# Fused forgetting attention and SwiGLU FFN: q and k of the first four head pairs in two column parts, their first gate sums by TensorE, and a new order of the first loads

## The chip, the cores and the metric

The kernel runs on one core of a Trainium2 chip. The core has five engines with instruction streams of their own: TensorE (PE, matrix products), VectorE (DVE), ScalarE (ACT), GpSimd (POOL) and SyncE (SP, which here only issues transfers). Transfers between DRAM and the on-chip memory are issued by SP, ACT or POOL and carried by 16 DMA engines. The metric is device time in microseconds (us) of one execution; lower is better.

## The reference

Causal attention with a forget gate for 8 batches, 8 heads, 576 positions and head size 64, followed by a feed-forward block over the 4608 tokens of 512 features, inner size 1536.

```python
scores = q @ k.T / sqrt(64)
cum    = cumsum(log(clip(f, 1e-4, 1)), axis=-1)         # per batch and head
scores = where(causal, -1e9, scores + cum[:, :, :, None] - cum[:, :, None, :])
attn   = softmax(scores) @ v
x      = attn with the heads of a token side by side    # 4608 x 512
out    = (silu(x @ w_gate) * (x @ w_val)) @ w_out
```

In a row of the scores the term of the row itself is the same for every column and drops out of the softmax, so only the sums of the columns are added.

## The kernel before

The work unit of attention is a pair of heads, 32 in all, four per batch. A pair's 576 query rows are cut into nine blocks of 64. Blocks 0 to 3 are the pair's first half (g = 0), blocks 4 to 8 its second half (g = 1). Block i needs the first 64(i + 1) columns of k. The two heads of a pair stand side by side in the 128 rows of every score tile.

For each pair the kernel does the following. `load_pair` brings q and k in as float32 (`kf`, `qf`, two buffers each), k in 96 partitions and q in 72, one transfer each, together with the gate sums `cb`: two transfers, one per head, each spreading one row of 576 sums over 64 partitions. `prepare` casts k and q to bfloat16 (L438, L436, L434), has TensorE transpose them in six and eight pieces (L452) and copies the results out of PSUM into `kt` and `qz` (L464, L466); q's copies are two, one per head. `scores` lets TensorE multiply a block (L498) and add the causal mask through an identity product (L502). VectorE adds `cb` and takes the minimum of the row in one instruction (L526), ScalarE does the exponential and its sum (L546). `normalize` scales the weights to bfloat16 tiles `pk` on POOL (L582); for pairs 0 to 7 TensorE transposes them (L612, copied out at L617), for later ones a transposing DMA does. `weighted` multiplies them with v (`vt`, L638), and `spread` copies the result into `xT` (L662), the FFN's input, a ring of 2560 tokens.

v comes in five chunks of 128 rows per batch (`load_v`, L678), each for all heads, through the float32 buffers `vf`, of which there are two, and is cast to `vt` (L682). The weights of the FFN come through POOL's queue with a cast, in four column pieces each for `wg` and `wv` (L695) and three pieces for `wo` (L699).

The gate sums of all 64 head rows are made once in the tile `fa` (buffer `t`): clamp (L366), logarithm (L368) and running sum (L369). The sums are stored to DRAM (`cum_f`, L378) and every pair's `cb` is read back from there (L418). Only pair 0 (`NSEL = 1`) goes another way: `select` multiplies `fa` with a 0/1 matrix `one` on TensorE (L393, in float32) and copies the result to `cb` (L397).

The FFN works on token tiles, the first two of 256 tokens. 256 tokens are the first halves of the four pairs of a batch, so tile 0 needs g = 0 of pairs 0 to 3, and tile 1 takes in their second halves. `gate` (L720) streams the tokens against `wg` and `wv`, ScalarE and VectorE combine them (L726, L728, L731), `project` (L748) multiplies with `wo`, and ScalarE or VectorE copies out (L755, L757).

The order on every engine is planned at build time. Each operation is declared with `pl.op`: engines it may run on with an assumed cost, the keys it reads and writes, a priority. `Plan.order` is a list scheduler: it takes the operation that can start soonest by its model and gives buffers in turn. `HEAD` lists the order of the first eight halves as pair and half, `at` holds each half's place in it, `NUDGE` shifts priorities of single units, `STARTUP` gives the order of the first loads: `p3` is q and k of pair 3, `f9` the gates, `c2` the sums of pair 2, `v01` chunk 1 of batch 0, `wv4` the piece of `wv` that starts at 128-column block 4. The load with number n in that list waits for the one that is `AHEAD` places ahead, and POOL's for the one `BEHIND` places ahead; within a queue transfers go out in order, so that one which waits for its buffer holds the ones behind it.

Of the kernel before, what the change touches and what calls it, by code (L numbers as in the profile page):

```python
# [194 lines left out]
def mm(*cols):  # L195
    return sum(max(29, c / 2.4 + 2.5) for c in cols)
# [3 lines left out]
def kernel(  # L200
# [46 lines left out]
    NDIRECT = 0  # L247
    NSEL = 1
    MOST = (("p", 1), ("o", 2), ("f", 3))
    AHEAD = 7  # L250
# [13 lines left out]
    NUDGE = "a10.0:1 a13.0:2 a15.0:-1 a15.1:-0.5 a16.1:-2 a20.0:-1 a21.0:1 a23.1:-1 a26.1:0.5 a27.1:-1.5 a28.0:1 a29.0:1 a31.1:10 f3:-4 f4:-7 f5:1 f6:2 f7:4.5 f8:4 f9:8 o6:-2.5 o8:2 q11:-2 q15:4 q22:5.5 q24:2.5"  # L264
# [34 lines left out]
    bufs("cm", [P, NB, QB], F32, 2)  # L299
# [11 lines left out]
    bufs("vf", [P, H, D], F32, 2)  # L311
# [24 lines left out]
    one = sb.tile([BH, 2 * max(NSEL, 1), 64], F32)  # L336
    setup({"POOL": 160 + 110 * NSEL}, lambda e: nc.gpsimd.tensor_copy(one, ident[0:BH, 0:2 * max(NSEL, 1)].unsqueeze(2).to_broadcast((BH, 2 * max(NSEL, 1), 64))),
# [36 lines left out]
    for p in range(NDIRECT):  # L374
# [5 lines left out]
    pl.op({"ACT": 1400}, lambda e: nc.scalar.activation(tiny[:, 1:2], tiny[:, 0:1], AF.Exp),  # L380
          [(("cb", p), 2) for p in range(NDIRECT)] + [("fa", 2), "ln"], ["exp"], -95)


    def select(p):
        pl.key(("cb", p), "cb", p)
        for n in range(2):
            a, z = S // 2 * n, S // 2 * (n + 1)
            bk = ("cs", p, n)
            pl.key(bk, "gv", line="c")

            def mult(e, p=p, bk=bk, a=a, z=z):
                w = one[:, 2 * p:2 * p + 2, :].rearrange("b h r -> b (h r)")
                nc.tensor.matmul(pl.buf(bk)[:, 0:z - a], w, pl.buf("fa")[0:BH, a:z], start=True, stop=True)  # L393
            pl.op({"PE": mm(4 * (z - a))}, mult, [("fa", 3), "one"], [bk], -98.5 + 3 * p, lat=220, holds=["fa"])

            def evac(e, p=p, bk=bk, a=a, z=z):
                (nc.scalar.copy if e == "ACT" else nc.vector.tensor_copy)(pl.buf(("cb", p))[:, a:z], pl.buf(bk)[:, 0:z - a])  # L397
            pl.op({"ACT": 370, "DVE": 385}, evac, [bk], [("cb", p), (("cb", p), 3)], -98.5 + 3 * p)
# [70 lines left out]

    def epool(i):  # L470
        return f"e{i}" if i % 2 == 0 else "eo"
# [13 lines left out]
    def scores(p, g):  # L485
# [3 lines left out]
        for n, bank in enumerate(BANKS[g]):  # L489
# [14 lines left out]
            pl.op({"PE": mm(*cols)}, mult, [("kt", p), ("qz", p), (("kt", p), "done"), (("qz", p), "done"), "mask"], [sk], pr, lat=220)  # L504
# [8 lines left out]
            for i, a, z in cuts:  # L513
# [18 lines left out]
                r = [sk, ("cm", p) if own else (("cb", p), 3)] + ([("m", p, i, "part")] if a and not two else [])  # L532
# [337 lines left out]
```

## Time and profile before

| | |
|---|---|
| median of 3 runs | 420.01 us (419.38 to 426.64) |
| the profiled execution | 420.02 us |
| its span, first to last instruction | 418.2 us |
| PE busy | 398.1 us (95%) |
| DVE busy | 325.3 us (78%) |
| ACT busy | 311.0 us (74%) |
| POOL busy | 252.6 us (60%) |
| first score matmul | 13.72 us |
| first add of gate sums on DVE (L526) | 17.63 us |
| first FFN matmul (L720) | 34.83 us |
| moved by DMA | 72.22 MB, mean 173 GB/s |

A page of the profile shows one execution. Its second part cuts the span into 40 slices of 10.5 us and gives each engine's busy share in tenths. Its chain follows the last instruction back to what released it, step by step. An answer on windows gives, for each stretch, the busy time of each engine and the number of its instructions in brackets, then the granted TensorE clock, the DMA share and the rate in GB/s. A timeline row has start, duration, engine, line, operation, tiles written and read, and in square brackets the idle time ahead of it with what ended it. SPq, ACTq and POOLq rows are issues of transfers: their duration is the issuing engine's, not the transfer's. Busy time of PE is modelled from pipelined instructions and is no measure of how much it streams.

### The profile page before, as it was taken

The page shows a single profiled execution, that of the slowest core. Times are in us where ns is not written, and L with a number is a line of the kernel's source. Part 1 is how long each engine was busy: PE and PEld are TensorE (multiplying, and loading weights), DVE is VectorE, ACT ScalarE, POOL GpSimd, SP SyncE. Part 2 cuts the span into 40 slices and gives each one's busy share as a digit, 9 for nine tenths or more (in the row PEclk, how much of TensorE's full clock was granted, in tenths as well). Part 3 has the DMA queues.
Part 4 walks back from the last instruction along what each step waited for, and adds up shares of the span by engine and source line. Part 5 has one row for each costly group of instructions (what it writes and reads, how often), then busy time and mean ns, then how long its engine had stood idle before and what let it go on. Part 6 is the DMA issues. An engine that isn't in the chain of part 4 may idle for free.

```text
span 418.2 us, 9999 instructions
## 1 busy us (share of the span) xinstructions
PE 398.1 (95%) x3304; PEld 231.8 (55%) x3304; DVE 325.3 (78%) x1044; ACT 311.0 (74%) x875; POOL 252.6 (60%) x460
## 2 busy tenths in 40 slices
PE   1679999999999999999999999999999999999996
PEld 1446887665555555555555555555454444447875
DVE  4589999989998979889998979898866474553532
ACT  4689999999999978888987979899886332223321
POOL 7399977999788983886795787759784000000000
PEclk9999999999999999999999999999999999999999
DMA  7999999997999999999999999979976401001111
GB/s 176 203 166 235 220 214 206 224 236 183 204 229 212 232 197 237 204 237 199 225 216 226 228 235 210 234 189 208 221 155 146 88 2 51 25 27 50 52 52 52
DMA packets 143029, 72.22 MB, mean 173 GB/s; under 512 B 117761, under 2 KB 129793, under 8 KB 142977
## 3 DMA queue, kind: packets, MB, share of 16 engines
q1 hardware_dynamic: 136804, 66.27, 73.8%
q0 software_dynamic: 5808, 4.72, 7.7%
q10 hardware_dynamic: 364, 0.59, 0.6%
q8 instruction: 26, 0.43, 0.4%
q14 instruction: 27, 0.21, 0.2%
HBM read 47.04 MB, written 9.58 MB: 135 GB/s over the span
## 4 chain that ended last, share of the span: by engine, by line
PE 77%; DMA 7%; ACT 6%; POOL 4%; DVE 3%; issue 2%; SPq 0%; POOLq 0%; DVEq 0%; ACTq 0%
PE gv L720 38%; PE gv L748 20%; PE sp L498 8%; PE tx L638 5%; DMA kf<-in_k_dram 3%; PE tx L452 3%; POOL pk L582 3%; PE gv L612 2%; DMA pT<-pk 2%; DVE t L526 2%; ACT eo L546 2%; ACT e L546 2%; PE sp L502 1%; DMA cb<-cum_f 1%; DMA cum_f<-t 1%
## 5 line engine op out<-in xcount | busy, mean ns | idle before, releaser
L526 DVE CUSTOM_DVE_ANT_0 t<-sp,cb 128x512 f32<-128x512 f32 (+7 forms) x288 | 130.9, 475 | 13.5 <-PE sp L502 5.0
L582 POOL TENSOR_SCALAR pk<-e,lr 128x128 bf16<-128x128 f32 (+3 forms) x190 | 100.1, 530 | 32.7 <-DVE lr L564 15.1
L720 PE MATMUL gv<-xT,wv 128*128 128x512 bf16 (+2 forms) x576 | 111.4, 326 | 0.0
L720 PE MATMUL gv<-xT,wg 128*128 128x512 bf16 (+2 forms) x576 | 111.3, 326 | 0.0
L728 DVE SCALAR_TENSOR_TENSOR th<-th,gv 128x512 f32<-128x512 f32 x108 | 73.9, 685 | 43.7 <-ACT th L726 43.2
L748 PE MATMUL gv<-wo,hh 128*128 128x512 bf16 (+1 forms) x444 | 107.5, 374 | 0.0
L726 ACT ACTIVATE th<-gv 128x512 f32<-128x512 f32 x108 | 64.0, 592 | 42.1 <-PE gv L720 40.3
L546 ACT ACTIVATE e<-t,tm 128x448 f32<-128x448 f32 (+4 forms) x160 | 88.5, 555 | 4.6 <-DVE tm L526 3.9
L731 DVE TENSOR_TENSOR hh<-th,gv 128x512 bf16<-128x512 f32 x108 | 73.4, 685 | 9.0 <-PE gv L720 5.5
L498 PE MATMUL sp<-kt,qz 128*128 128x448 bf16 (+6 forms) x320 | 72.8, 295 | 3.8 <-DVE tm L526 3.7
L582 POOL TENSOR_SCALAR pk<-eo,lr 128x256 bf16<-128x256 f32 (+3 forms) x128 | 67.7, 530 | 12.4 <-DVE lr L564 4.9
L546 ACT ACTIVATE eo<-t,tm 128x256 f32<-128x256 f32 (+3 forms) x128 | 71.2, 557 | 4.3 <-DVE tm L526 2.2
L720 PEld LDWEIGHTS <-wv 128*128 128x128 bf16 x576 | 49.3, 98 | 34.8
L720 PEld LDWEIGHTS <-wg 128*128 128x128 bf16 x576 | 49.2, 98 | 35.0
L748 PEld LDWEIGHTS <-hh 128*128 128x128 bf16 x444 | 39.7, 98 | 37.1
L502 PE MATMUL sp<-mask,ident 128*128 128x64 bf16 x288 | 48.2, 197 | 0.0
L755 ACT ACTIVATE ot<-gv 128x512 f32<-128x512 f32 (+1 forms) x33 | 19.1, 581 | 36.7 <-PE gv L748 34.7
L498 PEld LDWEIGHTS <-qz 128*128 128x128 bf16 x320 | 31.0, 101 | 19.8 <-DVE qz L466 1.3
L436 POOL TENSOR_SCALAR qb<-qf 72x1024 bf16<-72x1024 f32 x30 | 31.2, 1041 | 8.8 <-DMA qf<-in_q_dram 6.1
L502 PEld LDWEIGHTS <-ident 128*128 128x128 bf16 x288 | 27.2, 100 | 15.2 <-issue 3.9
L546 ACT ACTIVATION_READ_ACCUMULATOR e<-t,tm 128x1 f32 x160 | 30.7, 192 | 0.0
L638 PE MATMUL tx<-pT,vt 128*64 128x320 bf16 (+4 forms) x448 | 29.4, 266 | 0.7 <-DMA pT<-pk 0.3
(60 smaller groups left out, 379.7 us busy)
## 6 DMA issues: line engine op xcount, KB each, us to landing
out_dram<-ot SPq DMA_DIRECT2D x35, 256.0 KB
kf<-in_k_dram SPq DMA_DIRECT2D x31, 288.0 KB
qf<-in_q_dram SPq DMA_DIRECT2D x31, 288.0 KB
cb<-cum_f SPq DMA_DIRECT2D x62, 144.0 KB
vf<-in_v_dram SPq DMA_DIRECT2D x32, 256.0 KB
wo<-in_moe_w_out_dram POOLq DMA_DIRECT2D x3, 512.0 KB, 9.2
vf<-in_v_dram SPq DMA_DIRECT2D x8, 128.0 KB
wv<-in_moe_w_val_dram POOLq DMA_DIRECT2D x2, 512.0 KB, 8.3
```

The costliest lines, as they stand in the source:

```text
L436: eng[e].tensor_scalar(dst, src, -scale, 1.0, op0=ALU.mult, op1=ALU.mult)
L498: nc.tensor.matmul(sp[:, o:o + z - a], qz[:, i, :, :].rearrange("p h r -> p (h r)"), kt[:, a:z], start=True, stop=not last or p >= MFROM)
L502: nc.tensor.matmul(sp[:, o - QB:o], ident, mask, start=False, stop=True)
L526: nc.vector.tensor_tensor_reduce(out=pl.buf(tk)[:, a:z], in0=pl.buf(sk)[:, o:o + z - a], in1=pl.buf(("cm", p))[:, i, :] if own else pl.buf ...
L546: nc.scalar.activation(pl.buf(ek)[:, :L], pl.buf(tk)[:, :L], AF.Exp, bias=pl.buf(("tm", p, g))[:, 0, i:i + 1], scale=-1.0, accum_out=pl.bu ...
L582: eng[e].tensor_scalar(dst, src, r, 1.0, op0=ALU.mult, op1=ALU.mult)
L638: nc.tensor.matmul(xo[r, 0:QB * n], vt[:, c, 2 * hp + h, :], pT[:, a:a + n, 64 * h:64 * h + 64], start=(c == 0), stop=(c == nch - 1))
L720: nc.tensor.matmul(pl.buf(bk)[:, j * n:j * n + n], wt[:, ko, fc * P:fc * P + P], xT[:, ko, x0:x0 + n], start=ko == 0, stop=ko == KD - 1)
L726: pl.op({"ACT": 487}, lambda e, u=u: nc.scalar.activation(pl.buf(("th", t, u)), pl.buf(("wg", t, u)), AF.Tanh, scale=0.5), [("wg", t, u)], ...
L728: pl.op({"DVE": 605}, lambda e, u=u: nc.vector.scalar_tensor_tensor(pl.buf(("th", t, u)), pl.buf(("th", t, u)), 1.0, pl.buf(("wg", t, u)), ...
L731: pl.op({"DVE": 605}, lambda e, u=u: nc.vector.tensor_mul(pl.buf(("hh", t, u)), pl.buf(("th", t, u)), pl.buf(("wv", t, u))), [("u", t, u), ...
L748: nc.tensor.matmul(pl.buf(bk)[:, 0:z - a], hh[:, (fc % nf) * n + ms * P:(fc % nf) * n + ms * P + P], wo[:, fc, a:z], start=fc == 0, stop=f ...
```

## The change

The columns of q and k of pairs 0 to 3 are cut at `CUT` = 256 into part A (blocks 0 to 3) and part B (the other 320 columns). `parts` lists the pieces. For pairs 0 and 1 together, and 2 and 3 together, part A of k, part A of q and part B of k are one piece each, with the two pairs one below the other in the partitions (64 each); part B of q is a piece per pair (80 partitions). `load_parts` issues one transfer per pair and piece, part A of pairs 0 and 1 from ACT and the others from SP. `prepare_parts` casts a piece in one instruction, transposes it in four or five pieces and copies each pair's share out. A first half waits for parts A alone, a second half for both (`pair_done`, `cb_done`).

`select` now takes one part: part A of the gate sums of pairs 0 to 3 (`NSELA`) and part B of pair 0 come from TensorE; part B of pairs 1 to 3 is read back from DRAM, 320 columns instead of 576. The matrix `one` grows from 2 to 8 head rows.

The first eight halves start with pair 0 instead of pair 1; the second halves stay in the order 1, 0, 3, 2. The first loads have a new order, in which `k0` and `q1` are parts B, and `AHEAD` is 10 instead of 7. An unused pool `cm` goes, `vf` has three buffers instead of two, the load of the exponential's table gets a bias of 1000 in the planner, and `NUDGE` has new values throughout the kernel.

```diff
     JFROM = 8
     TWO = True
     NDIRECT = 0
+    NHALF = 4
+    NSELA = 4
     NSEL = 1
+    CUT = QB * (HI[0] + 1)
     MOST = (("p", 1), ("o", 2), ("f", 3))
-    AHEAD = 7
+    AHEAD = 10
     BEHIND = 6
     BOTH = 8
     LATER = {"DVE": 100}
@@ -257,11 +262,11 @@
...
-    STARTUP = "p0 f9 p1 c1 p3 p2 c2 v00 c3 wv0 wg2 wg0 wv2 v04 wv4 v01 v03 c4 wg4 v02 p4 wg8 wv8 v10 f0 p5 p6 c5 v14 c6 wo0 p7 wo4 v12 v13 v11 c7 wo8"
-    HEAD = "10 00 20 30 11 01 31 21"
...
+    STARTUP = "p0 f9 k0 p2 wv0 wg0 c0 v01 q1 q0 wv2 wg2 c1 v02 v00 k2 v04 c3 q2 wv4 v03 wg4 q3 c2 p4 v11 c4 wg8 wv8 c5 v14 p5 v13 v12 p6 c7 v10 c6 wo0 wo4 wo8 p7"
+    HEAD = "00 10 20 30 11 01 31 21"
...
-    bufs("cm", [P, NB, QB], F32, 2)
...
-    bufs("vf", [P, H, D], F32, 2)
+    bufs("vf", [P, H, D], F32, 3)
...
-    one = sb.tile([BH, 2 * max(NSEL, 1), 64], F32)
-    setup({"POOL": 160 + 110 * NSEL}, lambda e: nc.gpsimd.tensor_copy(one, ident[0:BH, 0:2 * max(NSEL, 1)].unsqueeze(2).to_broadcast((BH, 2 * max(NSEL, 1), 64))),
+    one = sb.tile([BH, 2 * NSELA, 64], F32)
+    setup({"POOL": 160 + 110 * NSELA}, lambda e: nc.gpsimd.tensor_copy(one, ident[0:BH, 0:2 * NSELA].unsqueeze(2).to_broadcast((BH, 2 * NSELA, 64))),
...
-    pl.op({"ACT": 1400}, lambda e: nc.scalar.activation(tiny[:, 1:2], tiny[:, 0:1], AF.Exp),
...
-    def select(p):
...
+    o.bias = {"ACT": 1000}
+    def select(p, part, a, z):
+        bk = ("cs", p, part)
+        pl.key(bk, "gv", line="c")
+        def mult(e):
+            w = one[:, 2 * p:2 * p + 2, :].rearrange("b h r -> b (h r)")
+            nc.tensor.matmul(pl.buf(bk)[:, 0:z - a], w, pl.buf("fa")[0:BH, a:z], start=True, stop=True)
+        pr = at[p, 0] - 1.2 if part == "A" else at[p, 1] - 1
+        pl.op({"PE": mm(4 * (z - a))}, mult, [("fa", 3), "one"], [bk], pr, lat=220, holds=["fa"])
+        def evac(e):
+            (nc.scalar.copy if e == "ACT" else nc.vector.tensor_copy)(pl.buf(("cb", p))[:, a:z], pl.buf(bk)[:, 0:z - a])
+        pl.op({"ACT": (z - a) * .833 + 130, "DVE": (z - a) / .96 + 85}, evac, [bk], [("cb", p), (("cb", p), part)], pr)
+    def cb_done(p, g):
+        return [(("cb", p), x) for x in ("A", "B")[:g + 1]] if p < NHALF else [(("cb", p), 3)]
+    def pair_done(p, g):
+        if p >= NHALF:
+            return [("kt", p), ("qz", p), (("kt", p), "done"), (("qz", p), "done")]
+        return [(("kt", p), x) for x in ("A", "B")[:g + 1]] + [(("qz", p), x) for x in ("A", "B")[:g + 1]]
...
+        if p < NHALF:
+            load_parts(p)
+            return
...
-        if NDIRECT <= p < NSEL:
-            select(p)
-        elif p >= NSEL:
+        if p >= NSEL:
...
+        if p < NHALF:
+            prepare_parts(p)
+            return
...
+    def parts(p):
+        if p % 2 == 0:
+            yield "k", "A", 0, CUT, 4, 2
+            yield "q", "A", 0, CUT, 4, 2
+            yield "k", "B", CUT, S, 5, 2
+        yield "q", "B", CUT, S, 4, 1
+    def load_parts(p):
+        b, hp = divmod(p, NPB)
+        pl.key(("cb", p), "cb", p)
+        for name, x, a, z, r, n in parts(p):
+            fk = (name + "f", p, x)
+            pl.key(fk, name + "f")
+            m = (z - a) // r
+            def load(e, fk=fk, src=(k if name == "k" else q), a=a, z=z, r=r, n=n, m=m):
+                for u in range(n):
+                    h0 = 2 * (hp + u)
+                    (nc.scalar if e == "ACT" else nc.sync).dma_start(
+                        out=pl.buf(fk)[m * u:m * u + m, :, 0:r * D],
+                        in_=src[b, h0:h0 + 2, a:z].rearrange("h (p r) d -> p h (r d)", r=r))
+            loads[name, p, x] = pl.op({"ACT" if p == 0 and x == "A" else "SP": 550 * n}, load, (), [fk], -99 + 3 * p, dma=n * (z - a) * 2)
+        for x, a, z, sel in (("A", 0, CUT, NSELA), ("B", CUT, S, NSEL)):
+            if p < sel:
+                select(p, x, a, z)
+                continue
+            for h in range(2):
+                loads["cb", p, x, h] = pl.op({"SP": 600}, lambda e, h=h, a=a, z=z: nc.sync.dma_start(
+                    out=pl.buf(("cb", p))[64 * h:64 * h + 64, a:z],
+                    in_=cum_dram[2 * p + h:2 * p + h + 1, a:z].to_broadcast((64, z - a))),
+                    ["cum_dram"], [(("cb", p), x)], -98.5 + 3 * p, dma=z - a, holds=[("cb", p)])
+    def prepare_parts(p):
+        for name, x, a, z, r, n in parts(p):
+            fk, bk, tk = (name + "f", p, x), (name + "b", p, x), ("tt", name, p, x)
+            m = (z - a) // r
+            pr = min(at[p + u, x == "B"] for u in range(n)) - 1 + (name == "q") * .1
+            pl.key(bk, name + "b")
+            pl.key(tk, "tx", line="q")
...
+            L = 2 * r * D
+            o = pl.op({"POOL": L + 60, "ACT": L * .833 + 210, "DVE": L * .62 + 60}, cast, [fk], [bk], pr)
+            o.bias = SPARE if p else {}
+            oks = [(("kt" if name == "k" else "qz"), p + u) for u in range(n)]
+            if x == "A":
+                for ok in oks:
+                    pl.key(ok, ok[0])
+            def transpose(e, bk=bk, tk=tk, r=r, w=m * n):
+                src = pl.buf(bk).rearrange("p r h d -> p r (h d)")
+                for j in range(r):
+                    nc.tensor.transpose(half(tk)[:, w * j:w * j + w], src[0:w, j, :], ident[0:w, 0:w])
+            pl.op({"PE": r * (m * n / 2.4 + 2.5)}, transpose, [bk], [tk] + (oks if x == "A" else []), pr, lat=200, holds=oks)
+            for u in range(n):
+                for lo, hi, h in ([(0, P, None)] if name == "k" else [(0, 64, 0), (64, 128, 1)]):
+                    def evac(e, lo=lo, hi=hi, h=h, u=u, tk=tk, ok=oks[u], a=a, z=z, r=r, n=n, m=m):
+                        src = half(tk)[lo:hi, 0:r * m * n]
+                        if h is None:
+                            src = src.rearrange("c (j u p) -> c u p j", j=r, u=n)[:, u, :, :]
+                            dst = pl.buf(ok)[lo:hi, a:z].rearrange("c (p j) -> c p j", j=r)
+                        else:
+                            src = src.rearrange("c (j u i p) -> c u i p j", j=r, u=n, i=(z - a) // QB)[:, u, :, :, :]
+                            dst = pl.buf(ok)[lo:hi, a // QB:z // QB, h, :].rearrange("c i (p j) -> c i p j", j=r)
+                        if e == "ACT":
+                            nc.scalar.copy(dst, src)
+                        else:
+                            nc.vector.tensor_copy(dst, src)
+                    pl.op({"ACT": (z - a) * .85 + 125, "DVE": (z - a) * 1.15 + 90}, evac,
+                          [tk] + ([("z", "qz", p + u)] if h is not None and p + u < len(pl.pools["qz"]) else []),
+                          [(oks[u], x)], at[p + u, int(x == "B")] - .9, holds=[oks[u]])
...
-            pl.op({"PE": mm(*cols)}, mult, [("kt", p), ("qz", p), (("kt", p), "done"), (("qz", p), "done"), "mask"], [sk], pr, lat=220)
+            pl.op({"PE": mm(*cols)}, mult, pair_done(p, g) + ["mask"], [sk], pr, lat=220, holds=[("kt", p), ("qz", p)])
...
-                r = [sk, ("cm", p) if own else (("cb", p), 3)] + ([("m", p, i, "part")] if a and not two else [])
+                r = [sk] + ([("cm", p)] if own else cb_done(p, g)) + ([("m", p, i, "part")] if a and not two else [])
...
+        elif x[0] == "p" and n < NHALF:
+            line += [loads["k", n, "A"], loads["q", n, "A"]]
+        elif x[0] in "kq":
+            line.append(loads[x[0], n, "B"])
+        elif x[0] == "c" and n < NHALF:
+            line += [loads["cb", n, y, h] for y in "AB" for h in range(2) if ("cb", n, y, h) in loads]
```

More of the change, by code (lines that the diff above doesn't have):

```diff
@@ L379 @@
           [("fa", 3)], ["cum_dram"], -120, dma=570, lat=0, holds=["fa"])
-    pl.op({"ACT": 1400}, lambda e: nc.scalar.activation(tiny[:, 1:2], tiny[:, 0:1], AF.Exp),
+    o = pl.op({"ACT": 1400}, lambda e: nc.scalar.activation(tiny[:, 1:2], tiny[:, 0:1], AF.Exp),
           [(("cb", p), 2) for p in range(NDIRECT)] + [("fa", 2), "ln"], ["exp"], -95)
-    def select(p):
[L385 to L398, printed above, removed]
+    o.bias = {"ACT": 1000}
[16 more added lines that the diff above has]
+        return [(("kt", p), x) for x in ("A", "B")[:g + 1]] + [(("qz", p), x) for x in ("A", "B")[:g + 1]]
     def half(key):
@@ new lines, in prepare_parts, with cast @@
+    def prepare_parts(p):
[5 more added lines that the diff above has]
+            pl.key(tk, "tx", line="q")
+            def cast(e, name=name, fk=fk, bk=bk, r=r, w=m * n):
+                src = pl.buf(fk)[0:w, :, 0:r * D].rearrange("p h (r d) -> p r h d", d=D)
+                dst = pl.buf(bk)[0:w, 0:r, :, :]
+                if e == "ACT":
+                    nc.scalar.activation(dst, src, AF.Copy, scale=-scale if name == "q" else 1.0)
+                elif name == "q":
+                    eng[e].tensor_scalar(dst, src, -scale, 1.0, op0=ALU.mult, op1=ALU.mult)
+                else:
+                    eng[e].tensor_copy(dst, src)
+            L = 2 * r * D
[20 more added lines that the diff above has]
+                            dst = pl.buf(ok)[lo:hi, a // QB:z // QB, h, :].rearrange("c i (p j) -> c i p j", j=r)
+                        if e == "ACT":
+                            nc.scalar.copy(dst, src)
+                        else:
+                            nc.vector.tensor_copy(dst, src)
+                    pl.op({"ACT": (z - a) * .85 + 125, "DVE": (z - a) * 1.15 + 90}, evac,
+                          [tk] + ([("z", "qz", p + u)] if h is not None and p + u < len(pl.pools["qz"]) else []),
+                          [(oks[u], x)], at[p + u, int(x == "B")] - .9, holds=[oks[u]])
```

2 lines of the change are left out of this document (1 added, 1 removed).

## The prediction

> **What bounds the kernel now.** I read the page first: its span, the slices and the chain's shares.
>
> ```profile
> span 418.2 us, 9999 instructions
> ...
> PE   1679999999999999999999999999999999999996
> ...
> GB/s 176 203 166 235 220 214 206 224 236 183 204 229 212 232 197 237 204 237 199 225 216 226 228 235 210 234 189 208 221 155 146 88 2 51 25 27 50 52 52 52
> ```
>
> TensorE looks full from the fourth slice on. A busy share is not work, so I set its work against its best pace. The longest single-line piece of the whole chain's list in mid-kernel gives that pace.
>
> ```profile
> 187.15 4.32 PE gv L720 x20
> ```
>
> 4.32 us for 20 matmuls of 512 columns is 216 ns each, 0.42 ns per column. The FFN streams 4608 x 96 gate columns and 36 x 12 x 512 projection columns: 186.6 + 93.3 us. Attention, by the loops of the code, has per pair 2880 score, 576 mask, 1152 transpose and 1600 effective PV columns (the two heads run side by side: ten PV matmuls of 320 columns take 0.71 us), 84 us for 32 pairs. The on-chip transposes of eight pairs add 10.8. That is 375 us of work in 418.2, so some 43 us are lost. The windows say where.
>
> ```profile
> core 0: us, PE busy (x) PEld busy (x) DVE busy (x) ACT busy (x) POOL busy (x), PEclk, DMA share, GB/s
> 0.00:5.00 5.00, 0.00 (x0) 0.00 (x0) 1.90 (x8) 1.49 (x2) 4.11 (x27) 1.00 0.62 151
> 5.00:10.00 5.00, 1.52 (x8) 1.24 (x9) 3.27 (x4) 3.11 (x4) 3.36 (x8) 1.00 0.79 191
> 10.00:15.00 5.00, 4.15 (x39) 2.95 (x38) 1.79 (x3) 2.90 (x5) 1.77 (x3) 1.00 0.82 214
> 15.00:20.00 5.00, 2.74 (x32) 2.20 (x30) 3.50 (x12) 2.55 (x9) 1.79 (x2) 1.00 1.17 211
> 20.00:25.00 5.00, 2.56 (x25) 2.16 (x24) 4.34 (x30) 4.71 (x20) 3.53 (x8) 1.00 1.43 164
> 25.00:30.00 5.00, 4.45 (x24) 2.29 (x24) 4.41 (x20) 4.60 (x18) 4.91 (x11) 1.00 0.92 156
> 30.00:35.00 5.00, 4.17 (x41) 2.29 (x41) 4.96 (x18) 4.59 (x16) 4.96 (x10) 1.00 1.16 210
> ```
>
> VectorE (third pair of figures) does almost nothing until 17.6 us and is full from about 20 on. The first gate matmul starts at 34.83. Until then TensorE has streamed 19,600 effective columns, which is 8.2 us of work, so 26.6 of the 43 lost us lie ahead of the first gate. The chain of waits over the first 36 us names what holds VectorE back:
>
> ```profile
> 1.38 6.10 DMA kf<-in_k_dram
> ...
> 8.81 3.11 DMA cum_f<-t
> ...
> 12.45 5.02 DMA cb<-cum_f
> ...
> 17.63 0.39 DVE t L526
> ```
>
> The gate sums go out to DRAM and come back repeated over 64 partitions, 8.81 to 17.47, although the scan that makes them ended at 7.80 and the first scores were done at 14.7. After 17.63 the chain is VectorE and ScalarE until 34.58, then TensorE. The timeline shows the rest that I use:
>
> ```profile
> 6.45 1.35 DVE L369 TENSOR_TENSOR_SCAN t<-tiny,t 64x576 f32<-64x576 f32 x1 [0.29 <-ACT t L368]
> ...
> 9.07 2.29 PE L393 MATMUL gv<-t,one 64*128 64x288 f32 x4
> ...
> 10.43 0.40 ACT L397 COPY cb<-gv 128x288 f32<-128x288 f32 x1 [1.55 <-PE gv L393]
> ...
> 15.64 9.65 SPq L678 DMA_DIRECT2D vf<-in_v_dram  x3
> ```
>
> The last row is SP held from 16.94 to 24.89 at the third v load: both v buffers were full, and the copy that frees one ran on POOL at 24.26.
>
> **The change, part by part.** *Gate sums by TensorE.* Columns 0 to 255 for pairs 0 to 3, 256 to 575 for pair 0. By L393, 2.29 us for 576 columns is 4.0 ns per column: 1.02 us for each A part, 1.27 for the B part, 5.4 in all against 2.29. It falls where TensorE is idle; without that cover it would cost 3.1. Pair 0's sums stand at 7.80 + 0.1 + 1.02 + 0.2 of latency + 0.36 of copy = 9.5.
>
> *Two parts of q and k.* A parts of two pairs share one load, cast and transpose group. Per two pairs the casts fall from 3584 to 2688 elements per partition, the transposed columns stay 2304. The copies out are split, twelve more of some 0.1 us each, 1.2 us over VectorE and ScalarE ahead of 34; I count them in the VectorE stretch below. The loads go from 8 to 16 DMAs on k and q. SP gets six more, at the 0.31 to 0.57 us that its k and q issues took about 3 us; ACT four instead of two, at 0.39 and 0.67 about 1 us, which puts its table load from 1.87 to 2.9 and its end to 4.4, before VectorE's clamp ends at 5.71: nothing, and beyond 1.3 us of slip one for one.
>
> *When the first add starts.* k and q A of pairs 0 and 1 and f are 0.67 MB. The present start moved 0.75 MB by 5.0 us (151 GB/s), so q is there at about 5.5. Cast (half of POOL's 1.04), four transposes of 128 (0.5) and six copies of 0.38 on two engines (1.1) end at 8 to 8.5, the scores at 9. So the sums are last, and the first add starts near 9.8 instead of 17.63.
>
> *What is late next.* Four first halves took VectorE from 17.63 to 25.8, 8.2 us; from 9.8 that ends at 18 if k and q A of pairs 2 and 3 are there. They wait on SP for the first k buffer (about 6), and share the wires with wv0 and wg0: in by 12.7. So the next bound is v: PV of every pair needs v00 and v01. By the new plan 4.9 MB stand ahead of the end of v00 (0.52 + 0.15 + 0.33 + 0.52 of q, k, f, four weight pieces of 0.52, v01, q1, q0, c1, v02, v00). The windows above sum to 4.66 MB at 25 and 5.44 at 30, so 4.9 MB were moved at 26.5. The third v buffer takes away SP's stop, in which the rate was 164 and 156: at 200 it would be 24.5. I take 25.5. The cast is 0.60 us, four PVs (0.36 warm, 0.55 for eight) 1.5, the last copies 0.7: first gate at 28.4, between 27.4 and 30.
>
> *What that is worth.* By then TensorE has done less: four first halves, their transposes, some 1.6 second halves, 16,400 effective columns, 6.9 us. Lost ahead of the gate: 28.4 - 6.9 = 21.5, against 26.6. That is 5.1 us won, 3.5 to 6.1 over the gate's range.
>
> *The clock.* Mask matmuls took 0.26 us until 29.04 and 0.19 from 30.03, groups of six transposes 0.83 and 0.50. The granted share in the windows is 1.00 throughout, so it does not show this. If the pace rises only after dense work, the first gates at 28.4 may run slow. Dense work began at 24.98, and the rise came 4.5 us later; gates at half pace for as long would lose 2.3 us. An earlier rise would win perhaps 0.5. I take 0.5 lost, nearer to the low end, because the work ahead of the gates was already dense when it rose. The Trainium skill, page "TensorE: Matmul & The Clock Gate", Part 1, has the array at half rate until one window of about 3.4 us was busy; by it the loss would be at most 3.4 / 2 = 1.7 us, and the jump between 29.0 and 30.0 agrees with it.
>
> *Priorities and nudges.* Pairs from 4 on keep their code, loads and buffers. The losses after 34.8 are 43 - 26.6 = 16.4 us, end included. New nudges can move them either way; with no row for it I take zero, and 3 us either side.
>
> Sum: 420.0 - 5.1 + 0.5 = 415.4, about 415.5. The profiled execution took 420.02 with 418.2 in the span, and the median of the runs shown is 420.01, so nothing is to be converted.
>
> **The rivals.** *Won and given back, 418 to 422.* The attention of pairs 4 on is not started earlier: the first of their loads goes out at 32.45, and in the new plan also stands behind all pieces of pairs 0 to 3. If attention rather than TensorE paces the middle, the earlier gates only lengthen a later wait. For it: the chain from 202 to 227 runs through POOL, a k load and a transposing DMA, not TensorE. Against it: TensorE still streams 96 to 99% of its pace between 100 and 350. Price: the whole 5.1, so 420. It is also what comes out if halved loads move slower: at the 156 GB/s of 25 to 30, 4.9 MB take 31.4 us and the gate comes at 34.3. The Trainium skill, page "DMA: Bandwidth & Descriptors", Bandwidth, speaks against the split: it wants at least 1 MiB per DMA and gives 138 GB/s at 64 KB, 341 at 1 MB. Its rule is not what the first window shows, where pieces of 0.29 MB in parallel gave 151 to 214.
>
> *The second halves starve TensorE, 422 to 430.* k2, q3 and c3 stand behind v00 and, with wv4 and wg4, behind some 6 to 8 MB, 31 to 38 us at 215 GB/s; now pair 3's second half is scored at 34. Token tile 1 needs the second halves of all four pairs. Tile 0's FFN is 24 groups of 0.87 and 24 projections of 0.216, 26 us, cover from 28.4 to about 54, with attention in between to 60. Two second halves at 4 us of VectorE each, beside FFN work that fills half of it, end 16 us after q3. It decides when q3 lands after about 42; each us beyond costs one. At 50 it takes the 5.1 back and 3 more: 423; at 55, 428.
>
> *More than the start, under 411.6.* The stretch 34.8 to 100 loses 4 us to VectorE, which now is ahead; if that goes too, 411.
>
> *The change does not do what it says.* If pair 1's A sums still waited for DRAM, the first add would stay at 17.6 and the time at 420; its code gives them to TensorE, so this is inside the first rival.
>
> **How the numbers follow.** Forecast (411.6 to 418) 0.52, given back 0.20, starved 0.12, more than the start 0.16. The time is the forecast's, 415.5. The range takes in the given-back case, half of the starved one and most of the better one: 409 to 423. Two per cent is 8.4 us, about what a measurement of this kernel can tell from no change: faster by more needs under 411.6, 0.17; slower by more needs over 428.4, the far end of the starved case, 0.05; the rest, 0.78, lies within.
>
> **What would show it.** Right: first L526 add at 9 to 11, no wait for cum_f ahead of it; cum_f and its return off the chain of the first 30 us; L720 first at 27 to 30; SP without an 8 us stop at v. Wrong: first add near 17, or early with L720 still at 34 (loads); TensorE waiting for tx or xT between 45 and 65 (starved); equal start gain but longer gaps after 200 (given back).

## The result, and the profile after

The changed kernel takes 418.95 us (median, 417.40 to 420.18), the kernel before 420.68 (419.38 to 430.46), 20 runs each. The ratio is 0.9949, with an interval of 0.9928 to 0.9969. The profiled execution took 418.96 us with 417.2 in the span. Fourteen of the 20 executions before lie between 419.38 and 421.86 us, mean 420.3, and six between 424.43 and 430.46; against the fourteen alone the changed kernel's mean of 418.87 is 1.4 us less. So the change wins 1.4 to 2 us, not 4.5.

From the page after:

```profile
span 417.2 us, 9955 instructions
...
PE   1979999999999999999999999999999999999996
...
PEclk9998999999999999999999999999999999999999
```

The PE row looks nearly full from the second slice on, but that is a busy share and not work. The fourth slice of the granted clock is new: an 8. Windows of after (columns as in the prediction's fence; from here on line numbers are those of the changed kernel, where L622 is the add, L594 and L598 are scores and mask, L546 the transposes, L559 and L561 their copies, L708 and L713 the transposes of the softmax weights and their copies, L734 the product with v and L816 the gate):

```profile
15.00:20.00 5.00, 5.00 (x37) 3.39 (x36) 4.42 (x22) 4.34 (x20) 2.63 (x6) 1.00 1.29 247
...
25.00:30.00 5.00, 3.92 (x40) 2.19 (x39) 4.05 (x16) 4.47 (x13) 4.97 (x10) 1.00 0.97 197
30.00:35.00 5.00, 3.44 (x25) 1.99 (x24) 4.94 (x21) 4.64 (x15) 4.02 (x8) 0.81 1.16 220
```

VectorE (third pair) works 4.42 us from 15 to 20 instead of 3.50, the wires carry more (247 instead of 211 GB/s there, 197 instead of 156 from 25 to 30), and POOL (fifth pair) is full from 25 to 30. The timeline gives the two ends of the start. First the way to the first add:

```profile
6.25 0.63 ACT L530 ACTIVATE kb<-kf 128x512 bf16<-128x512 f32 x1 [1.09 <-DMA kf<-in_k_dram]
6.78 0.67 ACT L372 ACTIVATE t<-t 64x576 f32<-64x576 f32 x1
...
8.25 1.34 DVE L373 TENSOR_TENSOR_SCAN t<-tiny,t 64x576 f32<-64x576 f32 x1
...
9.74 1.19 PE L395 MATMUL gv<-t,one 64*128 64x256 f32 x2 [2.20 <-DVE t L373]
...
11.50 1.51 ACT L559 COPY qz<-tx 64x256 bf16<-64x256 bf16 x4 [1.39 <-PE tx L546]
...
14.20 0.42 DVE L622 CUSTOM_DVE_ANT_0 t<-sp,cb 128x256 f32<-128x256 f32 x1 [1.13 <-PE sp L598]
```

The first add comes at 14.20 instead of 17.63, and no DRAM stands ahead of it. It does not come at 9.8. In ScalarE's order the logarithm (L372) stands behind the cast of k, which waited 1.09 us for k. On VectorE the copies of k stand ahead of the scan, which starts 0.8 us after the logarithm's end and ends at 9.59 instead of 7.80. TensorE then multiplies the sums before it transposes q (10.86), whose cast had ended at 8.59, and all four copies of q are on ScalarE, until 13.01. The add waits for the scores. Then the way to the first gate:

```profile
22.08 0.61 POOL L778 CAST vt<-vf 128x512 bf16<-128x512 f32 x1
...
28.64 0.56 DVE L713 COPY pT<-gv 128x768 bf16<-128x768 bf16 x1 [0.61 <-PE gv L708]
...
31.97 0.49 DVE L561 COPY qz<-tx 64x320 bf16<-64x320 bf16 x1
32.52 0.36 PE L734 MATMUL tx<-pT,vt 128*64 128x256 bf16 x4 [0.20 <-DVE qz L561]
33.39 0.49 DVE L561 COPY kt<-tx 128x320 bf16<-128x320 bf16 x1
34.30 1.91 PE L816 MATMUL gv<-xT,wg 128*128 128x256 bf16 x8
```

v was there at 22.7, earlier than forecast, and three first halves were multiplied by 26.7. The fourth had its softmax weights ready at 29.20 but started at 32.52, 0.06 us after the end of the copy at 31.97, which freed one of the two PSUM buffers `tx`: the transposes of parts B of pairs 2 and 3 held them. The first gate comes at 34.30, only 0.53 us earlier than the 34.83 of before.

Where the 3.4 us of the earlier add went is seen by windows cut at the first add and at the first gate. Before, then after:

```profile
0.00:17.63 17.63, 6.05 (x51) 4.43 (x52) 8.13 (x15) 8.14 (x12) 10.57 (x37) 1.00 0.82 191
17.63:34.83 17.20, 13.36 (x116) 8.55 (x114) 15.89 (x74) 15.65 (x57) 13.68 (x28) 1.00 1.15 179
```

```profile
0.00:14.20 14.20, 5.07 (x22) 2.99 (x22) 6.11 (x15) 6.97 (x13) 10.05 (x36) 1.00 1.00 206
14.20:34.30 20.10, 16.29 (x131) 10.15 (x130) 18.24 (x81) 18.37 (x65) 15.43 (x31) 0.97 1.09 225
```

VectorE works 24.0 us up to the first gate in the one and 24.4 in the other. In the kernel before 8.13 of them lie ahead of the first add; after, 6.11. From add to gate it works 18.24 instead of 15.89 us and is idle 1.86 instead of 1.31: 3.43 - 2.35 - 0.55 = 0.53. The wait for DRAM had been cover for VectorE's preparation of the next pairs.

For the rest I count what TensorE lost: the time less the work it had issued by then, each weight load by the columns of its matmul at 512 columns in 216 ns, without the gate sums (the work of the whole execution is 374.5 us in both kernels). The last row is a second trace of the changed kernel, from the last experiment.

| lost by (us) | 34 | 40 | 60 | 100 | 200 | 300 | 350 |
|---|---|---|---|---|---|---|---|
| before | 26.2 | 26.5 | 28.4 | 31.6 | 34.9 | 38.4 | 39.6 |
| after | 26.1 | 27.3 | 29.2 | 31.4 | 34.5 | 36.9 | 38.5 |
| after, once more | 26.3 | 27.9 | 29.9 | 32.6 | 35.8 | 38.3 | 39.8 |

At 100 us the changed kernel is not ahead: 0.2 us in one trace, 1.0 behind in the other. What it wins, it wins after that: from 100 to 350 us it loses 7.1 and 7.2, the kernel before 8.0. In the code of that stretch only the nudges and the third v buffer are changed; the planned order differs there as well, since the planner builds it on the start. These are differences of about 1 us between single traces, and two traces of one kernel differ by as much at 100 us.

### The profile page after: what moved, and what is told of

It reads as the page before. It is cut to its first block, busy times and chain, and to the rows that moved or that the text cites. A ratio compares the mean times of both kernels' runs of the same rounds, so it can differ in the third digit from the quotient of the medians.

```text
span 417.2 us, 9955 instructions
## 1 busy us (share of the span) xinstructions
PE 398.3 (95%) x3250; PEld 232.3 (56%) x3296; DVE 328.9 (79%) x1065; ACT 310.3 (74%) x872; POOL 251.7 (60%) x459
## 4 chain that ended last, share of the span: by engine, by line
PE 86%; DVE 4%; issue 1%; ACT 0%
PE gv L816 43%; PE gv L844 22%; PE sp L594 9%; PE tx L734 6%; PE tx L467 3%; PE sp L598 2%; PE gv L708 2%; DVE t L622 1%; DVE pT L713 1%; DVE hh L827 1%; DVE th L824 1%; DVE qz L481 1%; DVE kt L481 0%; ACT ot L851 0%; DVE tm L622 0%
## 5 line engine op out<-in xcount | busy, mean ns | idle before, releaser
L622 DVE CUSTOM_DVE_ANT_0 t<-sp,cb 128x320 f32<-128x320 f32 (+7 forms) x288 | 130.4, 475 | 12.1 <-PE sp L598 8.6
L816 PE MATMUL gv<-xT,wg 128*128 128x512 bf16 (+2 forms) x563 | 110.6, 327 | 0.8
L816 PE MATMUL gv<-xT,wv 128*128 128x512 bf16 (+2 forms) x562 | 109.3, 324 | 0.9
L844 PE MATMUL gv<-wo,hh 128*128 128x512 bf16 (+1 forms) x425 | 104.2, 373 | 0.8
L824 DVE SCALAR_TENSOR_TENSOR th<-th,gv 128x512 f32<-128x512 f32 x108 | 73.9, 684 | 39.3 <-ACT th L822 38.3
L642 ACT ACTIVATE e<-t,tm 128x576 f32<-128x576 f32 (+4 forms) x160 | 88.7, 556 | 8.9 <-DVE tm L622 8.3
L642 ACT ACTIVATE eo<-t,tm 128x128 f32<-128x128 f32 (+3 forms) x128 | 71.1, 556 | 4.7 <-DVE tm L622 2.9
L594 PE MATMUL sp<-kt,qz 128*128 128x448 bf16 (+6 forms) x320 | 71.9, 293 | 1.5 <-DVE tm L622 1.4
L678 POOL TENSOR_SCALAR pk<-eo,lr 128x128 bf16<-128x128 f32 (+3 forms) x127 | 67.6, 532 | 5.4 <-DVE lr L660 3.1
L816 PEld LDWEIGHTS <-wg 128*128 128x128 bf16 x576 | 49.8, 98 | 35.7
L816 PEld LDWEIGHTS <-wv 128*128 128x128 bf16 x576 | 48.9, 98 | 33.7 <-issue 0.3
L598 PE MATMUL sp<-mask,ident 128*128 128x64 bf16 x288 | 48.0, 197 | 0.0
L594 PEld LDWEIGHTS <-qz 128*128 128x128 bf16 x320 | 30.9, 100 | 20.9 <-DVE tm L622 0.9
L851 ACT ACTIVATE ot<-gv 128x512 f32<-128x512 f32 (+1 forms) x31 | 17.9, 580 | 27.1 <-PE gv L844 26.2
L598 PEld LDWEIGHTS <-ident 128*128 128x128 bf16 x288 | 27.2, 100 | 12.6 <-issue 1.9
L734 PE MATMUL tx<-pT,vt 128*64 128x320 bf16 (+4 forms) x448 | 29.6, 266 | 1.9 <-DVE pT L713 1.3
L451 POOL TENSOR_SCALAR qb<-qf 72x1024 bf16<-72x1024 f32 x28 | 29.1, 1041 | 3.1 <-DMA qf<-in_q_dram 2.0
L642 ACT ACTIVATION_READ_ACCUMULATOR e<-t,tm 128x1 f32 x160 | 30.6, 192 | 0.0
```

The costliest lines, as they stand in the source:

```text
L451: eng[e].tensor_scalar(dst, src, -scale, 1.0, op0=ALU.mult, op1=ALU.mult)
L594: nc.tensor.matmul(sp[:, o:o + z - a], qz[:, i, :, :].rearrange("p h r -> p (h r)"), kt[:, a:z], start=True, stop=not last or p >= MFROM)
L598: nc.tensor.matmul(sp[:, o - QB:o], ident, mask, start=False, stop=True)
L622: nc.vector.tensor_tensor_reduce(out=pl.buf(tk)[:, a:z], in0=pl.buf(sk)[:, o:o + z - a], in1=pl.buf(("cm", p))[:, i, :] if own else pl.buf ...
L642: nc.scalar.activation(pl.buf(ek)[:, :L], pl.buf(tk)[:, :L], AF.Exp, bias=pl.buf(("tm", p, g))[:, 0, i:i + 1], scale=-1.0, accum_out=pl.bu ...
L678: eng[e].tensor_scalar(dst, src, r, 1.0, op0=ALU.mult, op1=ALU.mult)
```

## The experiments

Ratios are to the kernel before, with 95% intervals; diffs are against the changed kernel unless said otherwise. The theories: VectorE's work paces the start (V); the drop of the clock at 33 us costs the gain (C); the nudges of the middle make the measured gain (M); the late logarithm holds the start (L); an earlier gate is given back (G).

**Nudges of before in the changed kernel, and the other way round.**

```diff
-    NUDGE = "a5.0:-2 a8.0:1 a13.0:-1 a15.0:-2 ...
+    NUDGE = "a10.0:1 a13.0:2 a15.0:-1 a15.1:-0.5 ...
```

> The changed kernel with the nudges of the kernel before. The first 45 us of the plan are the same, so by both theories the first gate matmul comes at about 34.2 us. Theory M (what was won comes from the middle, where the new nudges act): the ratio to the kernel before is 1.000 to 1.010. Theory S (what was won comes from the start): 0.993 to 0.997, as with the whole change.

> The kernel before with the new nudges alone. Theory M in its strong form (the nudges win by themselves): ratio 0.995 to 0.998. M in its weak form (a set of nudges fits one start only): 1.000 to 1.010. Theory S: 0.998 to 1.002. First gate matmul at 34.8 by all.

| ratio (interval) | nudges of before | nudges of after |
|---|---|---|
| code of before | 1 | 1.0059 (1.0025 to 1.0093) |
| code of after | 1.0103 (1.0056 to 1.0149) | 0.9949 (0.9928 to 0.9969) |

The same change of code costs 1% under the one set of nudges and wins 1.1% under the other, and either set is worse on the other's start. So the nudges alone are no gain; they fit a start. In the first run the gate comes at 34.44, the loss by 180 us is 33.9 and by 200 it is 40.8. Windows, and TensorE's waits between 180 and 200, of the changed kernel with the nudges of before:

```profile
189.00:192.00 3.00, 1.85 (x10) 0.93 (x11) 2.35 (x6) 1.63 (x8) 3.00 (x7) 0.50 0.90 204
192.00:195.00 3.00, 3.00 (x19) 1.27 (x18) 1.06 (x5) 1.83 (x6) 3.00 (x7) 0.50 1.21 200
```

```profile
PE tx L734 <- DVE qz L481: 2.0, 1, 2.0
```

TensorE waits 2.0 us, until 189.82, for a copy of q on VectorE, the clock falls to one half for 6.8 us from 188.67, and the price of both is some 7 us. In the other run the loss jumps from 26.1 at 40 us to 32.3 at 50; its chain of waits there:

```profile
31.73 9.15 DMA vf<-in_v_dram
...
40.94 0.61 POOL vt L682
...
45.33 1.71 PE gv L720 x8
```

A chunk of v lands at 40.88 and holds the gates that stand behind it, at half clock from 43.3 to 50.1.

**Score matmuls of the second halves of pairs 0 to 3 done twice** (the first result is overwritten; the order is unchanged, and TensorE gets 8,960 columns, 3.8 us, of added work where it starves).

```diff
-                    nc.tensor.matmul(sp[:, o:o + z - a], ...
+                    for again in range(2 if p < NHALF and g == 1 else 1):
+                        nc.tensor.matmul(sp[:, o:o + z - a], ...
```

> The changed kernel in which TensorE does each score matmul of the second halves of pairs 0 to 3 twice, with the same plan. Theory C (the half-clock piece from 33.06 to 36.47 costs 1.7 us, and too little TensorE work in the 3.4 us before sets it off): no half-clock piece after 23 us, the first group of eight gate matmuls in 0.87 instead of 1.71 us, ratio 0.990 to 0.994. Rival (VectorE sets the pace there and the clock costs nothing, or the doubled work delays VectorE by as much): ratio 0.994 to 0.998.

Measured 0.9969 (0.9938 to 1.0001), 419.58 us. In the profiled execution the clock is at one half from 24.75 to 28.16 and full from then on, so no drop comes at 33; the first gate is at 34.57, and the time is no better. The other executions say it more plainly: ten of the 12 have a mean granted clock of 0.999 or 1.000, that is no such drop, and take 419.8 us on average, the two with one 419.7. All 20 of the changed kernel have at least one (0.988 to 0.996) and average 418.9. The run with the nudges of before shows it from the other side: its order is that of the changed kernel on every engine up to 45 us, its clock is at one half from 24.83 to 35.07, three times as long, and by 100 us it has lost 31.6, as much as after. C falls. What the added work cost the run can't separate from what the clock won: by 100 us TensorE had lost 28.4 us plus the added 3.8, 32.2, between the two traces of after (31.4 and 32.6).

**Transposes of parts B of pairs 2 and 3 held until the fourth first half is multiplied.**

```diff
+            if x == "B" and p >= 2:
+                late.append(o)
...
+    pv = [o for o in pl.ops if ("xo", 3, 0) in o.writes][0]
+    for o in late:
+        o.after.append(pv)
```

> The changed kernel with the transposes of parts B of pairs 2 and 3 held back until the weighted product of pair 3's first half is issued. Theory T (that product waits for one of two PSUM banks, which these transposes hold): it starts at 28.5 to 30 us instead of 32.5, the first gate matmul at 30 to 31.5 instead of 34.3, and work lost by 40 us falls from 27.2 to 24.5 to 26. Rival (it waits for VectorE or the v rows): gate at 33 or later. The plan behind the start changes with it, which moves the whole by 2 us either way: ratio 0.988 to 0.998.

Measured 1.0005 (0.9971 to 1.004), 420.92 us. The fourth product starts at 29.01 and the first gate at 31.27, 3 us earlier than in the changed kernel: the `tx` buffers are what held it. But nothing of it lasts. At 36 us TensorE has lost 24.5 (after: 26.9), at 60 already 30.6 (29.2), at 100 33.6 (31.4), and the time is above the range of 0.988 to 0.998. TensorE's waits from 36 to 62 us of this run:

```profile
PE sp L596 <- DVE tm L624: 2.3, 5, 1.0
PE gv L818 <- DMA wg<-in_moe_w_gate_dram: 1.2, 1, 1.2
```

The gates come before their weights have landed, and the scores wait for VectorE, which is busy 9.8 of 10 us from 40 to 50 and again from 50 to 60.

**VectorE's work: the adds of pair 0's second half done twice; adds of blocks 6 and 7 of pairs 0 and 1 left out.** The order of both is that of the changed kernel.

```diff
+                    for again in range(2 if (p, g) == (0, 1) else 1):
                         nc.vector.tensor_tensor_reduce(
```

```diff
+                    if p < 2 and i in (6, 7):
+                        return
...
```

> The changed kernel in which VectorE does every add of pair 0's second half twice (some 3.7 us more on VectorE between 25 and 33 us), with the same plan. Theory V (VectorE, not TensorE, paces the kernel from 14 us to about 90, so that work moved to it takes back what its earlier start won): work lost by 60 us rises from 29.1 to 31.5 to 33.5, and the ratio to the kernel before is 1.001 to 1.006. Rival (from the first gate on TensorE paces, VectorE has slack): lost by 60 us at most 30, ratio 0.994 to 0.998.

> The changed kernel, same plan, which leaves out the add of gate sums and the row minimum for blocks 6 and 7 of pairs 0 and 1 (the exponential reads the gate sums there instead): some 2.9 us less on VectorE between 24 and 34 us. Theory V (VectorE paces the stretch): first gate matmul at 31 to 32.5 instead of 34.3, work lost by 60 us down from 29.1 to 25.5 to 27.5, ratio 0.984 to 0.991. Rival (v, POOL or the order on TensorE sets the gate): gate at 33.5 or later, ratio 0.993 to 0.997.

VectorE's busy time is 332.8 us in the first and 326.6 in the second, against 328.9. With 3.9 us more the time is 424.30 us, ratio 1.0085 (1.0055 to 1.0115), above the range for V; that is 5.4 us more than the changed kernel by the medians, 5.7 by the ratios. The gate comes at 38.15, 3.85 later, and the loss by 60 is 33.0, as V has it. Windows of that run:

```profile
30.00:35.00 5.00, 2.12 (x12) 0.94 (x10) 4.82 (x19) 2.52 (x8) 1.87 (x4) 0.50 1.15 223
35.00:40.00 5.00, 3.92 (x24) 2.36 (x23) 4.66 (x19) 2.73 (x8) 3.38 (x6) 0.50 1.06 208
```

From 30 to 40 VectorE alone is nearly full: here every microsecond of it is paid, and the half clock from 25.12 to 42.19 may add to the price. With 2.3 us less the time is 417.74 us, ratio 0.9914 (0.9885 to 0.9942), and the gate comes at 33.41, 0.9 earlier; by 60 us TensorE has lost 27.4, by 100 29.6, 1.8 less than after. Gate and ratio lie between the two expectations, the loss by 60 is V's. The time falls by 1.2 us by the medians and 1.5 by the ratios, little more than half of what was taken away, and the intervals of this run and of the changed kernel overlap. The profiled execution has no half clock before 415 us, so the clock may have a part in what it wins. A window of that run says what stands in the way of more:

```profile
25.00:30.00 5.00, 3.79 (x37) 2.04 (x37) 3.09 (x12) 4.47 (x13) 4.97 (x10) 1.00 1.03 200
```

VectorE has room now (3.09 of 5 us), but POOL with its weight issues, casts and scalings is as full as it was, and the fourth product still starts 2.4 us after the copy of its softmax weights (28.97 to 31.38). V holds: VectorE's work, added or taken away, moves the gate, with POOL and the `tx` buffers right behind.

**k's first cast not on ScalarE, so that the logarithm need not stand behind it.**

```diff
+            if p == 0 and x == "A" and name == "k":
+                del engs["ACT"]
```

> The changed kernel with ScalarE barred from the first cast of k. Theory L (the logarithm of the gates waits 1.9 us on ScalarE behind that cast, which waits for k): logarithm at 5 us instead of 6.78, scan done by 8 instead of 9.59, first add of gate sums at 12 to 13 instead of 14.2. Rival (q sets the first add): still 14. For the whole: theory G (the plan behind the start decides, the earlier start is given back): ratio 1.000 to 1.010, with the first gate at 28 to 31.5 us and the work lost by 100 us no lower than 31. Rival (an earlier gate is kept): ratio under 0.993.

Measured 1.0102 (1.0035 to 1.0169), 425.41 us. The edit missed: the planner put a copy of k on ScalarE instead, and the logarithm started at 7.99, later than before. The first add still came at 12.98, since q's copies ended at 11.40, and the gate at 30.81. So L falls as the explanation by itself: with a later logarithm the add came earlier, and what decided was all that stood ahead of q's copies. The gate 3.5 us earlier is again lost, 34.8 by 100 us. Its chain of waits later holds one weight piece of 10.7 us, for which TensorE waits 1.2:

```profile
70.53 10.70 DMA wo<-in_moe_w_out_dram
```

**Only the sums by TensorE** (against the kernel before; the unused pool goes to make room), **and only the parts** (the changed kernel, A sums of pairs 1 to 3 from DRAM).

```diff
-    NSEL = 1
+    NSEL = 4
-    bufs("cm", [P, NB, QB], F32, 2)
```

```diff
-    NSELA = 4
+    NSELA = 1
...
-                    ["cum_dram"], [(("cb", p), x)], -98.5 + 3 * p, ...
+                    ["cum_dram"], [(("cb", p), x)] + [("cb", p)] * (x == "A"), -98.5 + 3 * p, ...
```

> The kernel before with the gate sums of pairs 0 to 3 all made by TensorE over all 576 columns, q and k whole. Some 9.2 us of TensorE at the pace of L393, 7 more than before, lie ahead of the transposes. By all theories the first add does not come before 17 us, since q and k are loaded and transposed whole behind it; ratio 1.000 to 1.015.

> The changed kernel with TensorE sums for pair 0 alone; part A of pairs 1 to 3 is read back from DRAM. The first add (pair 0) stays at 14.2 us. Theory P (the sums by TensorE are what lets the first halves run through): pair 1's adds wait for DRAM until 17 to 19, the last first half and the first gate come at 38 or later, ratio 1.010 to 1.030. Rival (v and the PSUM bank set the gate anyway): gate by 35, ratio 0.995 to 1.005.

Measured 1.0220 (1.0136 to 1.0303) and 1.0267 (1.0183 to 1.0350), two runs each. In the first the add comes at 20.1 and the gate at 40.57: with whole q and k on the old plan of loads the sums by TensorE alone do not bring the add forward. In the second pair 0 starts early (13.3), pair 1's adds follow at 19.3 and those of the other two at 33.0 and 35.2, behind sums that were not asked of DRAM before 24.5. The products come at 24.0, 24.4, 40.2 and 42.7 and the gate at 43.45, as theory P has it. Both kept nudges and a load order made for another start, so their times are no measure of a part by itself; the gates say more.

**The order of the second halves straightened, and POOL's loads let go closer together**, each with nudges fitted anew on the planner's own model.

```diff
-    HEAD = "00 10 20 30 11 01 31 21"
+    HEAD = "00 10 20 30 01 11 21 31"
-    NUDGE = ...
+    NUDGE = ...
```

```diff
-    BEHIND = 6
+    BEHIND = 5
-    NUDGE = ...
+    NUDGE = ...
```

> The changed kernel with the second halves in the order 0, 1, 2, 3 and nudges fitted to it in the planner; the model puts the first gate 1.9 us earlier than for the change and its end 0.3 us later. Theory G (an earlier gate is given back, the end is decided by the plan as a whole): ratio 0.993 to 0.999. Rival (the gate decides): 0.988 to 0.992.

> The changed kernel with the weights let out one place earlier (BEHIND 5 instead of 6) and nudges fitted to it in the planner; the model puts the first gate 2.0 us earlier and its end 0.8 us later than for the change. Theory G: ratio 0.994 to 1.000. Rival (the gate decides): 0.988 to 0.992.

Measured 1.0055 (1.0018 to 1.0093) and 1.0023 (0.9994 to 1.0052), above the ranges of both theories. Both have the gate 2.8 to 3.0 us earlier (31.51, 31.27) and have lost only 24.0 and 23.8 at 34 us, the best starts of the study, at full clock, and both are slower than the changed kernel. At 60 us they have lost 28.2 and 29.9 (after: 29.2), at 100 34.6 and 32.2. The chain of the second shows what took the gate's lead:

```profile
40.59 11.61 DMA wv<-in_moe_w_val_dram
```

A weight piece let go at 40.6 lands at 52.2, and TensorE waits 0.7 us for it, after 0.5 for a piece of `wg`; the scores wait another 1.7 for VectorE between 36 and 62. In the first, TensorE waits 2.1 us for one cast of v just ahead of 70 us, and 3.4 us of half clock follow from 70.0; it loses 4.2 us from 66 to 74. Nudges that the model liked did not hold on the chip either, so this is no proof that no plan keeps the lead.

**The changed kernel once more.**

> The changed kernel again, unaltered. If the half-clock piece belongs to the plan, it lies at 33 to 36.5 us again; if it depends on when the clock's windows fall, it lies elsewhere or is absent. Ratio 0.993 to 0.997 as before.

Measured 0.9930 (0.9898 to 0.9961), 419.10 us: the small gain is there again. Its clock drops to one half for 3.4 us from 34.05, 0.7 us ahead of its first gate at 34.71; in the first trace it dropped at 33.06, 1.2 ahead. All 32 executions of the changed kernel, these 12 and the 20 of the result, have at least one such drop, so it comes with this plan. Its place does not: the run with the nudges of before has the same order up to 45 us and its drop at 24.83. So neither half of the expectation holds by itself.

No other version that computes the whole output was faster than the changed kernel.

## Why the prediction was wrong

Its time was 3.5 us off and inside its range, but the gain that it explained, an early first gate, did not come, and the gain that came was counted at zero.

- *Sums at 9.5, first add at 9.8.* **This step failed first.** It took the scan's end of 7.80 over from the old trace and added the new pieces. In the new order the logarithm waits behind a cast that waits for k (1.0 us), the scan behind copies (0.8), q's transposes behind the sums (2.3 after the cast's end), and four copies share one engine (1.5): 14.20. The landings themselves were later as well, q at about 7.9 instead of 5.5. That the add would no longer wait for DRAM was right.
- *Four first halves 8.2 us.* 14.20 to 23.42, 9.2 us, with copies of parts B in between (0.42 to 0.88 us each): nearly right.
- *v is late next, there at 25.5.* Wrong the good way: cast by 22.69. The bytes ahead of it were right (4.9 MB forecast, 4.8 moved by 22.1), the rate was 233 to 255 GB/s instead of about 200. SP was held 4.5 us at its next three v loads instead of 9.7, and v and two weight pieces had gone out by 6.2 us; what the third buffer did by itself was not tried. The Trainium skill, page "DMA: Bandwidth & Descriptors", Bandwidth, wants 1 MiB per DMA; in this trace halves of 131 to 164 KB, with more transfers in flight, did not lower the rate (219 GB/s from 5 to 10 us against 191). How fast one such transfer is by itself, no run shows.
- *First gate at 28.4.* **The step that cost the forecast**: 34.30. After its adds the fourth first half still had to pass POOL (full from 25 to 30), its copy on VectorE (28.64) and a `tx` buffer (32.52), each shared with the second halves; with the `tx` buffers kept free the gate came at 31.27. The prediction priced this stretch as four products behind v, and never asked what VectorE had done during the DRAM wait that it took away. With 18.24 us of VectorE work between an add at 14.20 and the gate, the gate of this order would be near 32.4 even if VectorE never waited.
- *5.1 us won ahead of the gate are won for good.* Wrong by the runs that did bring the gate forward by 2.8 to 3.5 us: ratios 1.0005, 1.0102, 1.0055 and 1.0023. Weights, v and VectorE were due by the old time; it is not the clock, which was full in the last two up to 70 us.
- *The clock, 0.5 lost.* Its size came near by luck. The rise that it feared would come late came by 23 us, ahead of the gates (a mask matmul took 0.26 us at 21.6 and 0.19 at 25.3); then the granted clock fell, and the first eight gate matmuls took 1.71 us. Between 34 and 40 us the two traces lose 1.2 and 1.6 against 0.3 before, but that does not last, since VectorE paces that stretch.
- *Nudges, zero, 3 us either side.* The size was open and the bounds held, but this term, with the third v buffer, is where the gain came from: between 100 and 350 us the changed kernel loses 7.1 and 7.2 and the one before 8.0. Which of the new nudges does it, or whether the third v buffer has a part in it, was not tried.
- *The rivals.* "Won and given back" has the time (418 to 422), and the runs with an earlier gate show it given back, by 60 to 100 us and not in the gaps after 200 that were to be its sign; in the changed kernel itself little was won to begin with. Its other form, slow loads and a gate at 34.3, has the gate by chance: the loads were faster. "The second halves starve TensorE" is not seen: from 36 to 62 us TensorE's one listed wait is 0.3 us. "More than the start" is not seen either.

What stays open: what in the middle's plan makes its gain of about 1 us, and whether a plan exists that keeps an earlier gate.

## What to carry to other kernels

When a long wait is taken away, list what each engine did during it: that work is not gone, it moves behind the wait's end (2.35 of the 3.43 us here), and the gain is what the fullest engine of the next stretch leaves. Price an operation's start by what stands ahead of it on its in-order engine in the new order, waits for data included, not by its time in the old trace. In these runs an earlier start was not kept unless what the next stage needs (weights, values, buffers, VectorE) was early as well; and a hand-fitted order can fit one start alone, so undo such fits apart from the code before crediting either.

## What the hardware showed unexpectedly

The granted clock falls to one half in steps of about 3.41 us: 3.4 in the changed kernel, 6.8, 10.2 and 17.1 in others. TensorE did not stand still ahead of it. In the changed kernel, the window of the step before the drop (which is at 33.06 to 36.47, granted 0.50):

```profile
29.65:33.06 3.41, 1.90 (x18) 1.09 (x17) 3.25 (x14) 3.09 (x10) 2.48 (x5) 1.00 1.21 210
```

PE counts as busy 1.90 of 3.41 us there, and by its columns it streamed about a third of its best pace (0.30 to 0.36, as the matmuls at the step's edges are counted); in the two steps before that, at 0.37 to 0.43, the clock stayed full. The Trainium skill, page "TensorE: Matmul & The Clock Gate", Part 1, gives the half rate, a window of about 3.4 us and a return to half after an idle window; the length agrees with the trace, but the window here was thin, not idle.

The same order of work does not always meet the drop at the same place: at 33.06 and 34.05 us in the two traces of the changed kernel, at 24.83 in the run with the nudges of before, whose first 45 us are the same. Nor does the record show every slow stretch: up to 21.6 us a mask matmul takes 0.26 us at a granted 1.00, from 25.3 on 0.19.

What the drop costs depends on the stretch. Where VectorE paces, at the start, it costs nothing that lasts: by 100 us 31.6 us are lost with 10.2 us of half clock and 31.4 with 3.4. Where TensorE paces, it multiplies a stall: a wait of 2.0 us that ended at 189.8 us came with 6.8 us at half clock, 3.4 of work not done. Of the 35 executions of the kernel before that ran beside the repeat, the 27 with a mean granted clock of 0.999 or 1.000 took 420.8 us on average, the eight with 0.991 to 0.996 took 424.4; whether the drop or the stall ahead of it makes these 3.5 us, no trace here shows.
